# Small token tiles on TensorE: each strip of the array takes its own output columns instead of its own part of the contraction

## The chip, the cores and the metric

The kernel runs on one core of one Trainium2 chip. The metric is device time in microseconds of one execution; lower is better. Each number for a kernel is the median of several runs. Engines are named as the profile names them: PE is TensorE (PEld are its loads of the stationary operand), DVE is VectorE, ACT is ScalarE, POOL is GpSimd, SP is SyncE, which here issues most DMAs.

## What is computed

Sliding-window attention with four sink tokens, and behind it a mixture of experts with a two-level choice of one expert per token. All arrays are float32.

```python
batch, n_heads, seq, head_dim = (4, 8, 768, 64)
n_sink, window = (4, 128)
N, D, G, Eg, F = (3072, 512, 4, 4, 1024)
...
keep = is_sink | in_window
scores = np.where(keep, scores, -1000000000.0)
...
x = attn_out.transpose(0, 2, 1, 3).reshape(B * S, H * D)
...
h = np.maximum(xg[mask_e] @ w1[g, e], 0.0)
ye = h @ w2[g, e]
combined = g_w[mask_g][mask_e] * e_w[mask_e]
out[tok_idx] = combined[:, None] * ye
```

So 3072 tokens of 512 features go to 16 experts. An expert multiplies its tokens by `w1` (512 x 1024), takes the positive part, multiplies by `w2` (1024 x 512), and each row is scaled by the token's gate.

## The kernel before

The first 180 us or so hold the attention, the routing and the first expert. After that the kernel does one expert after another, in the order of the list `GROUPS`, largest first where ranks are named by size: `CAPT` gives the number of token places that the expert of each rank has (rank 3: 288, rank 8: 160, rank 14: 64, rank 15: 32). Some groups join a large and a small expert: `[3, 14]` and `[4, 15]`.

**Ordinary tiles.** Weights arrive as float32 chunks `rw` (128 x 1024, eight per expert), ACT rounds each to `whi`, and DVE subtracts to get the remainder `wlo`. Tokens, transposed by PE (`tp<-ident,xg`) and split the same way, lie in `un`. Layer 1 writes PSUM tiles `ph`, of which there are four buffers; ACT and DVE turn them into the hidden values (`hc`, `un`, `hq`). Layer 2 writes `po` (two buffers), ACT scales it by the gate into `ot`, and POOL scatters `ot` to the output rows.

**Small tiles.** Two kinds of tile hold too few tokens for that, and are multiplied in plain float32 directly from the raw chunk `rw`. One kind is the two small experts (`plain`: rank 14 with 64 tokens, rank 15 with 32), both layers. The other is the last 32 tokens of the six experts in `FEW` (ranks 3, 4, 8, 9, 10, 11), layer 2 only, from the hidden values `hq`; `rest_of` starts these, and half of the products come after the fourth hidden chunk of the tile beside them, the other half after that tile is done. With w tokens as the stationary operand a product uses w of the array's 128 columns. So `side_by_side` puts m = 128 / w products next to each other, one in each strip of w columns: strip j takes contraction chunks j, j + m, ... over all 512 output columns. Each strip ends with a partial sum of the whole output in its own partitions of PSUM, and the m partial sums have to be added: in layer 1 of a small expert ACT copies one and DVE adds the others into `hs` (lines 1018 to 1022 of the listing), in layer 2 ACT scales one into `ot` and DVE adds the others, scaled (`scalar_tensor_tensor`, lines 1072 and 1073). `hidden_t` then transposes `hs` for layer 2, in eight pieces of at most 64 rows, in two jobs.

**What sets the order.** Every instruction is kept in program order on its engine (`keep_in_program_order`, line 107). Work for the next group (transposing its tokens by `xpose`, fetching rows by `gather`, the transposes of `hidden_t`) lies in a list of jobs, `todo`. `pop_todo` counts steps of the current products and runs the next job when the count is due:

```python
        def pop_todo():
            plan["at"] += 1
            if plan["todo"] and plan["at"] >= plan["next"]:
                plan["next"] += plan["every"]
                plan["todo"].pop(0)()
```

The jobs go in pairs, and `every` is the number of counted steps `tot`, less a few, over the number of pairs. The jobs of weight splitting (`wjob`) are started by a clock that the program keeps, `spend`.

Of the kernel before, what the change touches and what calls it, by code (L numbers as in the profile page):

```python
# [10 lines left out]
F32 = mybir.dt.float32  # L11
# [4 lines left out]
AF = mybir.ActivationFunctionType  # L16
ALU = mybir.AluOpType
# [5 lines left out]
P = 128  # L23
# [4 lines left out]
DM = H * D  # L28
HP = H // 2
NDC = DM // P  # L30
G, EG, F = 4, 4, 1024
NE = G * EG
NFC = F // P
# [101 lines left out]
def moe_attention(tc, kqT, vN, vS, nsw, wgx, w1, w2, out):  # L135
    nc = Pinned(tc)
    v = nc.vector
    with ExitStack() as top, ExitStack() as att:
# [36 lines left out]
        def bank(pt):  # L175
            return pt.tile([P, 4, P], F32, name="tp")
# [11 lines left out]
        def spare():  # L188
            return tail[0].tile([P, 512], F32, name="ph")
# [48 lines left out]
        ident = const([P, P], F32, "ident")  # L238
# [231 lines left out]
        start = const([P, NE], F32, "start")  # L470
# [522 lines left out]
        def whole(*k):  # L993
            while k not in held:
                prefetch(RAW + RAWB)
                if k not in held and not wjob(True):
                    raise RuntimeError("weights out of order")
            return held[k][0]

        def side_by_side(outs, w, n, xs, ws, chunk):  # L1000
            m = P // w
            for k in range(0, n, m):
                kk = range(k, min(n, k + m))
                for u, out in enumerate(outs):
                    for j, c in enumerate(kk):
                        nc.tensor.matmul(out[j * w:(j + 1) * w], xs(c), ws(c, u), start=k == 0, stop=k + m >= n)
                for c in kk:
                    held.pop(chunk(c), None) if chunk(c) != chunk(c + 1) else None
                prefetch(RAW + RAWB)
                yield 0.46 * len(outs) * len(kk) * w / 64  # L1010

        def layer1_plain(q):
            T, r = q["T"], q["r"]
            q["hs"] = h = yp.tile([P, F], F32, name="hs", bufs=1)
            ph = [ps_h.tile([P, 512], F32, name="ph") for u in range(2)]
            yield from side_by_side(ph, T, NDC, lambda c: q["x"][:, c], lambda c, u: whole(1, r, c)[:, u * 512:(u + 1) * 512],
                                    lambda c: (1, r, c))
            for u in range(2):
                us = slice(u * 512, (u + 1) * 512)
                nc.scalar.copy(h[0:T, us], ph[u][T:2 * T])  # L1020
                for a in [a for a in range(0, P, T) if a != T]:
                    v.tensor_tensor(h[0:T, us], h[0:T, us], ph[u][a:a + T], ALU.add)

        def layer1_narrow(q):
            T, o, r = q["T"], q["o"], q["r"]
# [15 lines left out]
        def hidden_t(q, u):  # L1041
            T = q["T"]
            tx = bank(ps_t)
            for c in range(4):
                f = 4 * u + c
                nc.tensor.transpose(tx[:, c, 0:T], q["hs"][0:T, f * P:(f + 1) * P], ident[0:T, 0:T])
            if q["plain"]:
                if u == 0:
                    q["h"] = yp.tile([P, NFC, 64], F32, name="hr", bufs=1)[:, :, 0:T]
                nc.scalar.activation(q["h"][:, 4 * u:4 * u + 4], tx[:, :, 0:T], AF.Relu)  # L1050
                return
            drain(split_h(q, slice(4 * u, 4 * u + 4), tx[:, :, 0:T]))

        plan = {}
# [1 line left out]
# [5 lines that stand above are left out]
# [2 lines left out]
            yield from few_tokens(q, spare(), q["h"], q["T"], 0)  # L1063

        def few_tokens(q, po, h, T, jj):
            r = q["r"]
            yield from side_by_side([po], T, NFC, lambda f: h[:, f],
                                    lambda f, u: whole(2, r, f // 2)[:, (f % 2) * DM:(f % 2 + 1) * DM], lambda f: (2, r, f // 2))
            c = cg[r, jj]
            ot = yp.tile([P, DM], F32, name="ot", bufs=3)  # L1070
            nc.scalar.activation(ot[0:T], po[T:2 * T], AF.Copy, scale=c[0:T])
            for a in [a for a in range(0, P, T) if a != T]:
                v.scalar_tensor_tensor(ot[0:T], po[a:a + T], c[0:T], ot[0:T], ALU.mult, ALU.add)
            scatter(r, jj, T, ot)

        def scatter(r, jj, w, ot):
# [192 lines left out]
        for i, g in enumerate(PARTS):  # L1269
            nxt = PARTS[i + 1] if i + 1 < len(PARTS) else []  # L1270
            if i == 1:
                fetch(nxt)
            todo = []
            for k, q in enumerate(g):
                plan.update(todo=todo, at=0, next=2, every=2)
                if i == 0 and k == 0:
                    finish(ew)
                elif q["T"] > P:
                    finish(layer1_wide(q))
                elif q["plain"]:  # L1280
                    finish(layer1_plain(q))
                    todo = todo + [lambda q=q, u=u: hidden_t(q, u) for u in range(2)]
                else:
                    finish(layer1_narrow(q))
                    todo = todo + [lambda q=q, u=u: hidden_t(q, u) for u in range(2)]
            for f in todo if g[0]["T"] <= P else []:
                f()
                todo = []
            tot = NFC * sum((q["m"] + P - 1) // P for q in g if not q["plain"])
            if i == 0:  # L1290
                todo += [lambda: wait_for("x1"), lambda: None]
            todo += [lambda q=q, j=j: xpose(q, j) for q in nxt for j in range(q["nt"])]
            todo = [lambda fs=todo[k:k + 2]: [f() for f in fs] for k in range(0, len(todo), 2)]
            if i >= 1 and i + 2 < len(PARTS):
                todo = spread(todo, PARTS[i + 2])
            first = (4 if g[-1]["plain"] else 8) if len(g) > 1 else 2
            plan.update(todo=todo, at=0, next=first, every=(tot - first - 3) / max(1, len(todo)))
            if i == 0:
                plan.update(todo=todo[:1], next=2)
            if i + 1 == len(PARTS):  # L1300
                nc.gpsimd.drain()
                fv = nc.nc.values_load(novi[0:1, 1:2], min_val=0, max_val=MAXO)
            work = [(q, j) for q in g for j in range((q["m"] + P - 1) // P)]
            if g[-1]["plain"]:
                work.insert(1, work.pop())
            for q, j in work:
                finish(layer2_plain(q) if q["plain"] else layer2(q, j))
                if (j + 1) * P < q["m"]:
                    continue
                if i == 0 and q["r"] == 0 and not q["last"]:  # L1310
                    plan.update(todo=todo[1:], next=tot - 8, every=1.5)
            for f in plan["todo"]:
                f()
# [237 lines left out]
```

## Time and profile before

| | us |
|---|---|
| median of 3 runs | 503.58 (502.59 to 505.25) |
| the profiled execution, its own time | 505.41 |
| its span in the profile | 503.70 |
| PE busy | 483.3 |
| DVE busy | 376.9 |
| ACT busy | 328.6 |
| POOL busy | 160.8 |

A row of the profile gives engine, line, operation, output and inputs by the program's names (buffer numbers are left out), shapes as partitions x elements, and a count. Nearly all instructions have line 105, that of a helper, so tiles are told apart by name. A float32 product appears as two loads and two matmuls. Matmuls are pipelined, so the duration of one overlaps with the next; starts say how fast they go.

### The profile page before, as it was taken

The numbers are of one execution on the slowest core, as the hardware profiler recorded it, in microseconds if no ns is written. First come the engines' busy times: TensorE is split into PE (matmuls) and PEld (weight loads), VectorE is DVE, ScalarE is ACT, GpSimd is POOL, SyncE is SP. The second block draws the span as 40 slices with busy tenths as digits, with TensorE's granted clock in tenths as the row PEclk, the third lists the DMA queues.
The fourth block names the chain that finished last, engine by engine and source line by source line (L and its number), as shares of the span: only waits on it lengthen the run. The fifth ranks groups of instructions, "written<-read, shape, count | busy, mean of one in ns | idle before, by whom it ended". The sixth has DMA issues, their size and how long they took to land.

```text
span 503.7 us, 14620 instructions
## 1 busy us (share of the span) xinstructions
PE 483.3 (96%) x5399; PEld 403.1 (80%) x5399; DVE 376.9 (75%) x1175; ACT 328.6 (65%) x861; POOL 160.8 (32%) x276
## 2 busy tenths in 40 slices
PE   7998999999999999999999999899999999999994
PEld 5787888888888888989888659685768788988883
DVE  6474897899989789983174287676988888688881
ACT  4887788879895345762264276456577877677851
POOL 3564354554563012422303044120712170205021
PEclk8999999999999999999999999999999999999999
DMA  7767676877885559894123399549949996858100
GB/s 210 242 216 217 208 240 196 271 235 240 299 291 196 150 186 388 288 318 154 67 86 121 114 325 362 173 170 316 397 152 349 412 393 217 303 190 304 59 24 29
DMA packets 50000, 114.71 MB, mean 228 GB/s; under 512 B 9486, under 2 KB 9486, under 8 KB 49920
## 3 DMA queue, kind: packets, MB, share of 16 engines
q1 hardware_dynamic: 45424, 100.14, 58.3%
q0 software_dynamic: 4352, 13.26, 7.5%
q8 instruction: 44, 0.72, 0.6%
q10 hardware_dynamic: 144, 0.29, 0.3%
q14 instruction: 36, 0.29, 0.2%
HBM read 100.89 MB, written 13.24 MB: 227 GB/s over the span
## 4 chain that ended last, share of the span: by engine, by line
PE 72%; DVE 11%; issue 8%; ACT 5%; DMA 1%; POOL 1%; POOLq 0%; DVEq 0%; ACTq 0%
PE po L105 31%; PE ph L105 26%; PE ps L105 6%; PE tp L105 6%; ACT pt L105 2%; PE lg L105 2%; DVE wlo L105 2%; DVE sm L105 1%; ACT whi L105 1%; DVE ot L105 1%; DVE un L105 1%; DMA ni<-in_nsw 1%; POOL out L105 1%; DVE hs L105 1%; DVE ps L105 1%
## 5 line engine op out<-in xcount | busy, mean ns | idle before, releaser
L105 DVE TENSOR_TENSOR wlo<-rw,whi 128x1024 fp32r<-128x1024 f32 x112 | 134.5, 1223 | 25.0 <-ACT whi L105 24.4
L105 PE MATMUL ph<-un,whi 128*128 128x256 f32 (+4 forms) x576 | 132.3, 317 | 1.8 <-DVE hc L105 0.9
L105 PE MATMUL po<-whi,un 128*128 128x512 f32 (+2 forms) x384 | 127.1, 396 | 0.0
L105 ACT CAST whi<-rw 128x1024 fp32r<-128x1024 f32 (+1 forms) x116 | 115.4, 1021 | 8.0 <-PE po L105 4.7
L105 POOL DMA_INDIRECT out<-ot,sidx x33 | 43.9, 1330 | 225.4 <-ACT ot L105 156.4
L105 PE MATMUL ph<-un,wlo 128*128 128x160 f32 (+4 forms) x416 | 100.4, 266 | 0.0
L105 PEld LDWEIGHTS ph<-un,whi 128*128 128x128 f32 x576 | 94.5, 189 | 6.8 <-issue 1.7
L105 PEld LDWEIGHTS po<-whi,un 128*128 128x128 f32 (+1 forms) x384 | 70.8, 186 | 24.9 <-issue 2.5
L105 ACT ACTIVATE pt<-sm,st 128x136 f32<-128x136 f32 x192 | 76.0, 399 | 20.2 <-DVE st L105 20.1
L105 PE MATMUL po<-wlo,un 128*128 128x512 f32 (+3 forms) x200 | 78.0, 390 | 0.0
L105 PEld LDWEIGHTS ph<-un,wlo 128*128 128x128 f32 x416 | 77.1, 189 | 0.7
L105 POOL DMA_INDIRECT xg<-xd,gidx x33 | 39.0, 1183 | 35.7 <-DVE idz L105 25.2
L105 DVE CUSTOM_DVE_ANT_0 sm<-ps,msk 128x136 f32<-128x136 f32 x192 | 45.5, 295 | 3.7 <-PE ps L105 0.7
L105 PE MATMUL ps<-kb,qb 64*64 64x216 f32 (+1 forms) x768 | 41.4, 353 | 2.4 <-DMA qb<-in_kqT 2.1
L105 PEld LDWEIGHTS po<-wlo,un 128*128 128x128 f32 (+2 forms) x200 | 36.3, 182 | 7.4
L105 DVE TENSOR_TENSOR hc<-ph,hc 128x160 f32<-128x160 f32 (+2 forms) x64 | 21.9, 344 | 24.5 <-ACT hc L105 24.3
L105 ACT ACTIVATE un<-ph 128x256 fp32r<-128x256 f32 x40 | 15.4, 384 | 35.7 <-PE ph L105 35.4
L105 ACT ACTIVATION_READ_ACCUMULATOR pt<-sm,st 128x1 f32 x192 | 36.3, 189 | 0.0
L105 ACT ACTIVATE ot<-po,cg 128x512 f32<-128x512 f32 (+3 forms) x25 | 17.0, 679 | 28.0 <-PE po L105 27.9
L105 PEld LDWEIGHTS ps<-kb,qb 64*64 64x64 f32 x768 | 27.6, 139 | 9.2 <-issue 2.7
L105 ACT COPY hc<-ph 128x160 f32<-128x160 f32 (+2 forms) x64 | 19.9, 312 | 20.9 <-PE ph L105 17.5
L105 PE MATMUL po<-pa,vv 128*64 128x64 f32 x768 | 30.8, 223 | 1.6 <-issue 1.6
(199 smaller groups left out, 743.4 us busy)
## 6 DMA issues: line engine op xcount, KB each, us to landing
rw<-in_w SPq DMA_DIRECT2D x128, 512.0 KB, 5.4
vv<-in_vN SPq DMA_DIRECT2D x24, 512.0 KB, 4.5
kb<-in_kqT SPq DMA_DIRECT2D x23, 288.0 KB, 4.8
qb<-in_kqT SPq DMA_DIRECT2D x24, 256.0 KB, 4.5
xd<-xt SPq DMA_DIRECT2D x24, 256.0 KB, 2.9
svr<-in_vS SPq DMA_DIRECT2D x4, 192.0 KB, 5.3
xg<-xd,gidx POOLq DMA_INDIRECT x33, 5.2
out<-ot,sidx POOLq DMA_INDIRECT x33, 5.6
```

The lines of the kernel that those rows point to most:

```text
L105: r = f(*a, **k)
```

## The change

`side_by_side` now gives strip a of the array the output columns a·k to (a + 1)·k, with k = 512·w/128 (for layer 1, 1024·w/128), and runs it over every contraction chunk. The strips end with finished sums of different columns. A product of 32 tokens that was 512 columns wide becomes four of 128 columns, one of 64 tokens becomes two of 256 (in layer 1 of the 64-token expert the width stays 512, with both halves of the output in one PSUM tile). `layer1_plain` takes one PSUM tile instead of two and ends with one ACT copy; `hidden_t` transposes `hs` in 128-row pieces, four for 64 tokens and two for 32, and one ACT instruction puts them in place. In `few_tokens` ACT scales each strip into its columns of `ot`, and the additions on DVE are gone. Also, a half of the rest-products now counts as a step in `pop_todo`, and `tot` counts two steps for each of them.

```diff
-        def side_by_side(outs, w, n, xs, ws, chunk):
+        def side_by_side(out, w, n, k, xs, ws, chunk, plain=True):
             m = P // w
...
-                for u, out in enumerate(outs):
-                    for j, c in enumerate(kk):
-                        nc.tensor.matmul(out[j * w:(j + 1) * w], xs(c), ws(c, u), start=k == 0, stop=k + m >= n)
+                for c in kk:
+                    for a in range(m):
+                        nc.tensor.matmul(out[a * w:(a + 1) * w, 0:k], xs(c), ws(c)[:, a * k:(a + 1) * k], start=c == 0, stop=c == n - 1)
...
                 prefetch(RAW + RAWB)
-                yield 0.46 * len(outs) * len(kk) * w / 64
+                if n == NFC and not plain:
+                    pop_todo()
+                yield 0.46 * k * m / 512 * len(kk) * w / 64
...
-            for u in range(2):
-                us = slice(u * 512, (u + 1) * 512)
-                nc.scalar.copy(h[0:T, us], ph[u][T:2 * T])
-                for a in [a for a in range(0, P, T) if a != T]:
-                    v.tensor_tensor(h[0:T, us], h[0:T, us], ph[u][a:a + T], ALU.add)
+            nc.scalar.copy(h[:, 0:k], ph[:, 0:k])
...
+            if q["plain"]:
+                m = P // T
+                nb = NFC // m
+                for c in range(nb):
+                    nc.tensor.transpose(tx[:, c], q["hs"][:, c * P:(c + 1) * P], ident)
+                q["h"] = h = yp.tile([P, NFC, 64], F32, name="hr", bufs=1)[:, :, 0:T]
+                nc.scalar.activation(h.rearrange("p (a c) t -> p c a t", a=m),
+                                     tx[:, 0:nb].rearrange("p c (a t) -> p c a t", a=m), AF.Relu)
+                return
...
-            nc.scalar.activation(ot[0:T], po[T:2 * T], AF.Copy, scale=c[0:T])
-            for a in [a for a in range(0, P, T) if a != T]:
-                v.scalar_tensor_tensor(ot[0:T], po[a:a + T], c[0:T], ot[0:T], ALU.mult, ALU.add)
+            for a in range(P // T):
+                nc.scalar.activation(ot[0:T, a * k:(a + 1) * k], po[a * T:(a + 1) * T, 0:k], AF.Copy, scale=c[0:T])
...
-                    todo = todo + [lambda q=q, u=u: hidden_t(q, u) for u in range(2)]
+                    todo = todo + [lambda q=q: hidden_t(q, 0)]
...
-            tot = NFC * sum((q["m"] + P - 1) // P for q in g if not q["plain"])
+            tot = sum(NFC * ((q["m"] + P - 1) // P) + 2 * (q["m"] < q["T"]) for q in g if not q["plain"])
```

PE in layer 2 of rank 8, while the tokens of the next group `[4, 15]` are transposed (`xg` are the fetched token rows, `hq` the hidden values of the 32 rest tokens). Before:

```order
L105 MATMUL po<-whi,un 128x512
L105 MATMUL tp<-ident,xg 128x32 x8
L105 MATMUL ph<-rw,hq 32x512 x4
L105 MATMUL po<-whi,un 128x512
L105 MATMUL po<-wlo,un 128x512
```

With the change:

```order
L105 MATMUL po<-whi,un 128x512
L105 MATMUL ph<-rw,hq 32x128 x16
L105 MATMUL tp<-ident,xg 128x32 x8
L105 MATMUL po<-whi,un 128x512
L105 MATMUL po<-wlo,un 128x512
```

The first half of the rest-products, now sixteen narrow products in place of four wide ones, stands ahead of the transposes instead of behind them. The same exchange takes place in layer 2 of rank 9, with the transposes of a 128-token tile.

PE in layer 2 of `[4, 15]`, around the transposes of rank 15's hidden values `hs`. Before:

```order
L105 MATMUL po<-whi,un 128x512
L105 MATMUL tp<-ident,hs 128x32 x8
L105 MATMUL ph<-rw,hq 32x512 x4
L105 MATMUL po<-whi,un 128x512
```

With the change:

```order
L105 MATMUL po<-whi,un 128x512
L105 MATMUL tp<-ident,hs 128x128 x2
L105 MATMUL tp<-ident,xg 128x128 x4
L105 MATMUL ph<-rw,hq 32x128 x16
L105 MATMUL po<-whi,un 128x512
```

Eight transposes become two, and the transposes of the next group's 128-token tile, which stood after the products of rank 15, follow them at once.

DVE over the same stretch, from layer 1 of `[4, 15]` to layer 1 of rank 9, as the difference of the two programs:

```order
-L105 TENSOR_TENSOR hs<-hs,ph 32x512 x6
-L105 TENSOR_TENSOR wlo<-rw,whi 128x1024 x3
-L105 SCALAR_TENSOR_TENSOR ot<-ph,cg,ot 32x512 x3
-L105 TENSOR_TENSOR wlo<-rw,whi 128x1024
-L105 SCALAR_TENSOR_TENSOR ot<-ph,cg,ot 32x512 x3
-L105 TENSOR_TENSOR un<-tp,un 128x4x128
-L105 COPY cg<-xg 128x1
+L105 TENSOR_TENSOR un<-tp,un 128x4x128
+L105 COPY cg<-xg 128x1
+L105 TENSOR_TENSOR wlo<-rw,whi 128x1024 x2
 L105 TENSOR_TENSOR un<-tp,un 128x4x32
 L105 COPY cg<-xg 32x1
-L105 TENSOR_TENSOR wlo<-rw,whi 128x1024 x4
+L105 TENSOR_TENSOR wlo<-rw,whi 128x1024 x6
```

All twelve additions are gone; the eight weight splits are still there.

## Rows read from the trace of the kernel before

**Rows 1.** The page: its head, and the chain that ended last by engine.

```profile
span 503.7 us, 14620 instructions
...
PE 72%; DVE 11%; issue 8%; ACT 5%; DMA 1%; POOL 1%; POOLq 0%; DVEq 0%; ACTq 0%
```

**Rows 2.** Waits of PE, 282 to 400 us: total us, times, longest.

```profile
PE tp L105 <- DVE cg L105: 2.4, 3, 1.1
PE ph L105 <- DVE hc L105: 0.9, 2, 0.4
PE tp L105 <- DVE hs L105: 0.8, 1, 0.8
PE ph L105 <- DVE ot L105: 0.7, 1, 0.7
PE ph L105 <- DVE cg L105: 0.3, 1, 0.3
```

**Rows 3.** Busy time by stretch: PE, PEld, DVE, ACT, POOL, clock, DMA share, GB/s.

```profile
352.00:400.00 48.00, 45.15 (x259) 37.17 (x258) 42.59 (x88) 33.94 (x64) 14.51 (x10) 1.00 0.86 323
400.00:488.00 88.00, 88.00 (x506) 74.19 (x505) 74.06 (x145) 66.49 (x122) 23.66 (x16) 1.00 0.64 227
```

**Rows 4.** Timeline of layer 2 of `[4, 15]`: start, us, engine, instruction [idle before].

```profile
340.73 2.12 DVE L105 TENSOR_TENSOR hs<-hs,ph 32x512 f32<-32x512 f32 x3
...
342.90 0.43 PE L105 MATMUL tp<-ident,hs 32*128 32x32 f32 x4 [0.85 <-DVE hs L105]
...
343.26 1.07 PE L105 MATMUL ph<-rw,hq 128*32 128x512 f32 x8
```

**Rows 5.** Timeline of layer 2 of rank 8.

```profile
317.68 0.43 PE L105 MATMUL tp<-ident,xg 32*128 32x32 f32 x4 [1.13 <-DVE cg L105]
...
318.34 0.43 PE L105 MATMUL tp<-ident,xg 32*128 32x32 f32 x4 [0.23 <-DVE cg L105]
...
318.70 1.07 PE L105 MATMUL ph<-rw,hq 128*32 128x512 f32 x8
...
319.70 0.50 PE L105 MATMUL po<-whi,un 128*128 128x512 f32 x1
```

**Rows 6.** Timeline of rank 9 and of layer 1 of rank 6.

```profile
357.01 4.61 DVE L105 TENSOR_TENSOR wlo<-rw,whi 128x1024 fp32r<-128x1024 f32 x4
...
361.90 0.41 PE L105 MATMUL ph<-un,whi 128*128 128x320 f32 x1 [0.45 <-DVE hc L105]
...
371.82 0.65 PE L105 MATMUL tp<-ident,xg 128*128 128x128 f32 x4 [1.04 <-DVE cg L105]
...
381.75 0.41 PE L105 MATMUL ph<-un,whi 128*128 128x384 f32 x1 [0.65 <-DVE ot L105]
```

**Rows 7.** Instructions that write `ot`: duration ns min/median/max, first and last start, forms.

```profile
L105 DVE SCALAR_TENSOR_TENSOR ot<-ph,cg,ot x22: 732/745/754, 295.1 to 496.4; 32x512 f32<-32x512 f32 x21, 64x512 f32<-64x512 f32 x1
L105 ACT ACTIVATE ot<-ph,cg x9: 473/681/686, 294.4 to 494.9; 32x512 f32<-32x512 f32 x7, 64x512 f32<-64x512 f32 x1, 128x256 f32<-128x256 f32 x1
```

**Rows 8.** Timeline of the last rest-products (rank 11).

```profile
492.62 0.13 PEld L105 LDWEIGHTS ph<-rw,hq 128*32 128x32 f32 x4 [0.30 <-issue]
493.05 0.13 PEld L105 LDWEIGHTS ph<-rw,hq 128*32 128x32 f32 x4 [0.30 <-issue]
```

**Rows 9.** Loads of those products: duration ns min/median/max.

```profile
L105 PEld LDWEIGHTS ph<-rw,hq x96: 106/109/111, 289.2 to 493.1; 128*32 128x32 f32 x96
```

**Rows 10.** Timeline of the attention's 64-column products, two strips side by side.

```profile
100.89 0.64 PE L105 MATMUL po<-pa,vv 128*64 128x64 f32 x16
101.36 0.64 PE L105 MATMUL po<-pu,vv 128*64 128x64 f32 x16
```

**Rows 11.** Timeline of the end.

```profile
494.87 2.31 DVE L105 SCALAR_TENSOR_TENSOR ot<-ph,cg,ot 32x512 f32<-32x512 f32 x3 [4.12 <-ACT ot L105]
...
497.15 0.47 ACT L105 ACTIVATE ot<-po,cg 128x256 f32<-128x256 f32 x1 [1.81 <-PE po L105]
497.46 0.87 POOL L105 DMA_INDIRECT out<-ot,sidx  x1 [12.42 <-DVE ot L105]
498.63 0.99 POOL L105 DMA_INDIRECT out<-ot,sidx  x1 [0.30 <-issue]
```

More of the change, by code (lines that the diff above doesn't have):

```diff
@@ L998, in whole @@
             return held[k][0]
-        def side_by_side(outs, w, n, xs, ws, chunk):
+        def side_by_side(out, w, n, k, xs, ws, chunk, plain=True):
             m = P // w
-            for k in range(0, n, m):
-                kk = range(k, min(n, k + m))
-                for u, out in enumerate(outs):
-                    for j, c in enumerate(kk):
-                        nc.tensor.matmul(out[j * w:(j + 1) * w], xs(c), ws(c, u), start=k == 0, stop=k + m >= n)
+            for k0 in range(0, n, m):
+                kk = range(k0, min(n, k0 + m))
+                for c in kk:
+                    for a in range(m):
+                        nc.tensor.matmul(out[a * w:(a + 1) * w, 0:k], xs(c), ws(c)[:, a * k:(a + 1) * k], start=c == 0, stop=c == n - 1)
                 for c in kk:
@@ L1009, in side_by_side @@
                 prefetch(RAW + RAWB)
-                yield 0.46 * len(outs) * len(kk) * w / 64
+                if n == NFC and not plain:
+                    pop_todo()
+                yield 0.46 * k * m / 512 * len(kk) * w / 64
         def layer1_plain(q):
             T, r = q["T"], q["r"]
+            k = F * T // P
             q["hs"] = h = yp.tile([P, F], F32, name="hs", bufs=1)
-            ph = [ps_h.tile([P, 512], F32, name="ph") for u in range(2)]
-            yield from side_by_side(ph, T, NDC, lambda c: q["x"][:, c], lambda c, u: whole(1, r, c)[:, u * 512:(u + 1) * 512],
-                                    lambda c: (1, r, c))
-            for u in range(2):
-                us = slice(u * 512, (u + 1) * 512)
-                nc.scalar.copy(h[0:T, us], ph[u][T:2 * T])
-                for a in [a for a in range(0, P, T) if a != T]:
-                    v.tensor_tensor(h[0:T, us], h[0:T, us], ph[u][a:a + T], ALU.add)
+            ph = spare()
+            yield from side_by_side(ph, T, NDC, k, lambda c: q["x"][:, c], lambda c: whole(1, r, c), lambda c: (1, r, c))
+            nc.scalar.copy(h[:, 0:k], ph[:, 0:k])
         def layer1_narrow(q):
@@ L1046, in hidden_t @@
                 nc.tensor.transpose(tx[:, c, 0:T], q["hs"][0:T, f * P:(f + 1) * P], ident[0:T, 0:T])
[L1047 to L1051, printed above, removed]
             drain(split_h(q, slice(4 * u, 4 * u + 4), tx[:, :, 0:T]))
@@ L1065, in few_tokens @@
         def few_tokens(q, po, h, T, jj):
-            r = q["r"]
-            yield from side_by_side([po], T, NFC, lambda f: h[:, f],
-                                    lambda f, u: whole(2, r, f // 2)[:, (f % 2) * DM:(f % 2 + 1) * DM], lambda f: (2, r, f // 2))
+            r, k = q["r"], DM * T // P
+            yield from side_by_side(po, T, NFC, k, lambda f: h[:, f],
+                                    lambda f: whole(2, r, f // 2)[:, (f % 2) * DM:(f % 2 + 1) * DM], lambda f: (2, r, f // 2), q["plain"])
             c = cg[r, jj]
             ot = yp.tile([P, DM], F32, name="ot", bufs=3)
-            nc.scalar.activation(ot[0:T], po[T:2 * T], AF.Copy, scale=c[0:T])
-            for a in [a for a in range(0, P, T) if a != T]:
-                v.scalar_tensor_tensor(ot[0:T], po[a:a + T], c[0:T], ot[0:T], ALU.mult, ALU.add)
+            for a in range(P // T):
+                nc.scalar.activation(ot[0:T, a * k:(a + 1) * k], po[a * T:(a + 1) * T, 0:k], AF.Copy, scale=c[0:T])
             scatter(r, jj, T, ot)
```

## The prediction

> **What bounds the kernel now.** The page comes first: of the chain that ended last PE holds 72% and DVE 11% [rows 1]. So an operation taken off DVE is worth something only where PE, or the last output, waits for DVE. The second view is the list of PE's waits in the stretch in which small tiles are computed. It is short, and every entry names DVE: 2.4 + 0.9 + 0.8 + 0.7 + 0.3 = 5.1 us, five groups, eight waits [rows 2]. The third is busy time by stretch. From 352 to 400 us DVE works 42.59 of 48 us, from 400 to 488 PE is busy all of 88.00 us [rows 3]; what DVE saves in the later stretch shortens nothing there. The timelines then show what stands in each wait, and the end of the kernel has a queue of its own on POOL.
>
> **What the change does to the products.** It leaves the multiplications and the columns streamed through each strip as they were, and makes more and narrower instructions of them. Half of a 32-token contraction (call it a block: four chunks, four strips) was two passes of 512 columns in each strip and becomes eight of 128. There are 14 such blocks: two for each of the six rest tiles, two for layer 2 of rank 15. One pass of 512 columns takes 493.05 - 492.62 = 0.43 us [rows 8]. No row has 128 columns, so I bound it. From above: the attention's 64-column products, two strips at a time, start 16 in 101.36 - 100.89 = 0.47 us, 0.029 us each [rows 10]; if instructions can't be fed faster than that, the 32 of a block take 0.94 us against 2 x 0.43 = 0.86, 0.08 more. From below: strictly by columns, nothing more. Between: a straight line through 64 columns (0.47/8 = 0.059 in one strip) and 512 (0.43) gives 0.059 + 64 x 0.00083 = 0.112 for 128, 0.90 for a block, 0.04 more. I take the line, as both its ends are measured with strips running together: 14 x 0.04 = 0.5, and 0.1 for the 256-column products of the two small experts. **Cost 0.6 us, between 0 and 1.2.** [...]
>
> **What it takes off, place by place.**
>
> *Hidden values of rank 15.* DVE adds six partial sums; three take 2.12 us [rows 4]. PE stands 0.85 us before the second four of eight transposes, and that second four last until 343.26, another 0.36 us [rows 4]. Afterwards one ACT copy feeds two transposes; it starts when layer 1 ends, with four counted steps of layer 2 between, so it is not late. Gain 0.85 + 0.36 = **1.2 us** (0.85 to 1.3). For rank 14 the profile names no such wait: 0. The next tile's transposes move up in both groups; between nothing and 0.3 us for one interruption of layer 2 less, I take nothing.
>
> *Rank 8.* The transposes of the last small tiles wait 1.13 and 0.23 us for DVE to empty a PSUM tile [rows 5]. Only then does the first rest block run, from 318.70 to 319.70, 1.00 us. The change counts steps differently, and the block now stands ahead of these transposes: it runs in the wait. The transposes can start no earlier than now, but the ordinary products follow them at once. Gain **1.0 us** (0 if the DVE work moves along, 1.0 at most).
>
> *Rank 9.* The same exchange at a wait of 1.04 us [rows 6]. Gain **1.0 us** (same bounds). The transposed tile comes no earlier, while layer 1 after it does; a later wait there is part of the first rival.
>
> *Layer 1 of rank 6.* PE waits 0.65 us because the three additions of a rest tile stand ahead of `hc` on DVE [rows 6], 0.745 us each [rows 7]. They go. In their place ACT does four strips of 128 columns instead of one of 512. From 0.681 for 512 and 0.473 for 256 [rows 7] a line gives 0.37 for 128, so 4 x 0.37 - 0.68 = 0.8 us more on ACT, per rest tile. Queued behind it are ACT's own `hc` copy and weight casts. With four `ph` buffers PE can run ahead of that. Gain **0.6 us** (between 0.65 and a loss of 0.15, the 0.8 exposed).
>
> *Layer 1 of rank 9.* Two waits of 0.45 us for `hc` (one in [rows 6], the sum in [rows 2]) and one of 0.3 for `cg`. DVE is late there: four splits run back to back for 4.61 us [rows 6] after 6 x 0.71 + 6 x 0.745 = 8.7 us of additions in the group before [rows 4, 7], all of which go. But the splits also need weights that have landed, and DMA engines are at 0.86 [rows 3]. Of 1.2 us I take half, **0.6 us** (0 to 1.2).
>
> *The end.* POOL's second-last scatter starts at 497.46, 0.28 after DVE's last addition (494.87 + 2.31 = 497.18), and ends at 498.33. The last starts 0.30 later, though its data are ready at 497.15 + 0.47 = 497.62 [rows 11]. Without additions, ACT begins the rest tile about 0.68 ahead of DVE's first addition, at 494.2, ends four strips at 495.7 and so lets POOL run from 496.0 to 496.9. The last scatter then waits only for its data: 497.62 + 0.28 = 497.9 instead of 498.63. Gain **0.7 us** (0 to 0.7).
>
> Other removed additions lie where PE waits for nothing: 0, with PE's own products as cover. **Sum:** 1.2 + 1.0 + 1.0 + 0.6 + 0.6 + 0.7 - 0.6 = 4.5 us. The profiled execution took 505.41 us with a span of 503.70; less 4.5 that makes 500.9. It was 1.8 us slower than the median of the runs, 503.58, from which the same sum gives **499.1 us**, 0.9% less. A difference of 0.5%, 2.5 us, is about what a measurement can tell from none. With every upper bound the gain is 1.3 + 1.0 + 1.0 + 0.65 + 1.2 + 0.7 + 0.6, with no cost for narrow products, 6.4 us: 497.2.
>
> **Rivals.** *The waits move on.* PE gets ahead of DVE by the exchange alone, not by faster evictions, and may meet weights or ACT at the next place. For it: DVE at 42.59 and ACT at 33.94 of 48 us, DMA at 0.86 [rows 3], and 0.8 us more ACT work for each rest tile. Against it: no wait in [rows 2] names ACT or a DMA. Then the four gains at ranks 8, 9 and 6 (3.2 us) are given back, and 503.58 - (1.2 + 0.7 - 0.6) = 502.3 remains, between 501 and 503.
>
> *Loads become visible; the other sign.* Each strip now gets a new stationary tile for every 128 columns instead of 512: eight loads per block and strip, where there were two. If a strip's load waits for its own product, 0.109 us [rows 9] is exposed in each of 14 x 8 passes: 12.2 us, so 499.1 + 12.2 = 511.3. The 4.5 us are used up once 0.040 us of each load shows, and it is slower by over 0.5% from 0.063. [...]
>
> *Feeding binds.* [...] By the slowest feeding that rows show it costs 14 x 0.08 = 1.1 us, which is in my range; to be slower overall it would need 0.038 us per instruction instead of 0.029 [rows 10]. [...]
>
> *It does not do what it says.* The additions go, but the waits belong to something that the profile names wrongly, such as a transfer behind DVE's wait. Then gains and cost cancel: 503.6. Against it: at the places above DVE is seen working up to the end of PE's wait.
>
> **Chances.** Forecast 0.66, of which all is faster by over 0.5%; waits move on 0.20, of which 0.05 still faster and 0.15 the same; not what it says 0.06, the same; loads visible 0.06 and feeding 0.02, slower. So faster 0.71, same 0.21, slower 0.08. The range goes from 497.0, just below all upper bounds, to 502.8, which takes in most of the first rival; 0.08 + 0.06 and a little of the rival, some 0.17, lie outside. The forecast alone would reach from 497.0 to 501.0.
>
> **What would show it.** Right: `hq` blocks of about 0.9 us with 128-column matmuls some 0.11 apart in a strip; the transposes of rank 8 and 9 behind a block, with a wait under 0.4 us; two `hs` transposes without wait; no `ot` addition on DVE before `hc`; the last scatter starting within 0.3 us of its data. Wrong: blocks of 1.2 us or more, waits of PE for `whi`, `wlo` or ACT between 340 and 400 us, or a stretch from 400 to 488 us that has grown.

## The result and the profile after

The changed kernel takes **496.94 us** (median of four runs, 495.42 to 498.27) against 504.41 of the kernel before in the same comparison: ratio 0.9854, 95% interval 0.981 to 0.9898, so 7.5 us less. Forecast were 499.1 us, 4.5 less. The sign is as forecast; the size is not, and 496.94 lies 0.06 under the low end of the range. A later comparison found a smaller gain, 4.7 us; it comes under "Before, order and change once more".

The profiled execution took 497.12 us. Its page, to be held against [rows 1]:

```profile
span 495.4 us, 15313 instructions
...
PE 479.5 (97%) x5757; PEld 412.5 (83%) x5757; DVE 354.9 (72%) x1145; ACT 331.8 (67%) x879; POOL 154.9 (31%) x276
...
PE 76%; issue 7%; DVE 6%; ACT 5%; DMA 3%; POOL 1%; POOLq 0%; ACTq 0%; DVEq 0%
```

DVE's share of the chain has fallen from 11% to 6%. The waits of PE from 282 to 400 us, before five groups with 5.1 us [rows 2]:

```profile
PE ph L105 <- DVE hc L105: 0.4, 1, 0.4
PE tp L105 <- DVE cg L105: 0.2, 1, 0.2
```

Busy time by stretch, with the columns of [rows 3]. No wait went into the later stretch. From 352 to 400 us ACT works 39.09 us where it had 33.94, but these microseconds hold other work now that the kernel is ahead; over the whole kernel ACT has 331.8 us instead of 328.6:

```profile
352.00:400.00 48.00, 47.59 (x326) 40.97 (x325) 41.53 (x86) 39.09 (x73) 11.48 (x10) 1.00 0.92 351
400.00:488.00 88.00, 88.00 (x632) 77.09 (x631) 66.15 (x140) 62.65 (x125) 20.04 (x14) 1.00 0.54 193
```

Timeline of layer 2 of rank 8, which answers to [rows 5]. The 32 narrow products run where PE stood for 1.13 us, and the first four transposes follow them without a listed wait; by the starts 0.2 us of it is left (1.20 us from the block to the transposes, where a block takes 1.01). The wait of 0.23 us ahead of the second four is the one that stayed:

```profile
313.76 1.08 PE L105 MATMUL ph<-rw,hq 128*32 128x128 f32 x32
...
314.96 0.43 PE L105 MATMUL tp<-ident,xg 32*128 32x32 f32 x4
...
315.62 0.43 PE L105 MATMUL tp<-ident,xg 32*128 32x32 f32 x4 [0.23 <-DVE cg L105]
...
315.98 0.50 PE L105 MATMUL po<-whi,un 128*128 128x512 f32 x1
```

Timeline of PE in layer 2 of `[4, 15]`, which answers to [rows 4]: two `hs` transposes with no wait, and the next tile's transposes and the rest-products in one piece behind them.

```profile
337.58 0.39 PE L105 MATMUL po<-whi,un 128*128 128x512 f32 x1
337.81 0.38 PE L105 MATMUL tp<-ident,hs 128*128 128x128 f32 x2
338.03 0.60 PE L105 MATMUL tp<-ident,xg 128*128 128x128 f32 x4
338.56 1.08 PE L105 MATMUL ph<-rw,hq 128*32 128x128 f32 x32
339.57 0.50 PE L105 MATMUL po<-whi,un 128*128 128x512 f32 x1
```

From 338.56 to 339.57 are 1.01 us for a block (products are counted as the rows count them, two for one in float32); from 318.70 to 319.70 it was 1.00 with wide products [rows 5]. The end, which answers to [rows 11]:

```profile
485.51 1.98 ACT L105 ACTIVATE ot<-ph,cg 32x128 f32<-32x128 f32 x5 [3.76 <-PE ph L105]
...
487.27 0.88 POOL L105 DMA_INDIRECT out<-ot,sidx  x1 [12.10 <-ACT ot L105]
...
488.51 0.47 ACT L105 ACTIVATE ot<-po,cg 128x256 f32<-128x256 f32 x1 [1.02 <-PE po L105]
489.26 1.00 POOL L105 DMA_INDIRECT out<-ot,sidx  x1 [1.11 <-ACT ot L105]
```

The last scatter starts 489.26 - 488.98 = 0.28 us after its data, where it was 1.01 [rows 11].

**Place by place.** The table below is read from the starts of PE's products: the time from one stage's first product to the next stage's, in microseconds. The last column, called the measure in the expectations, runs from the first layer-2 product of `[3, 14]` to the first product behind the last rest tile. It leaves out the start and the end of the kernel, whose durations vary between executions. The rows for the experiments are used below; a repeat stands as "again".

| kernel | [3,14] L2 | 8 L2 | [4,15] L2 | 9 L1 | 9 L2 | 6 L1 | measure |
|---|---|---|---|---|---|---|---|
| before | 18.89 | 10.98 | 18.46 | 9.76 | 10.55 | 15.70 | 208.4 |
| after | 18.54 | 10.00 | 16.62 | 8.88 | 9.37 | 14.78 | 202.2 |
| order alone | 18.85 | 9.99 | 18.12 | 10.59 | 9.37 | 15.70 | 206.7 |
| products alone | 18.75 | 12.55 | 16.67 | 8.25 | 10.58 | 14.77 | 205.5 |
| layer 2 and order | 18.92 | 10.00 | 18.19 | 9.90 | 9.37 | 14.78 | 205.1 |
| layer 1 and order | 18.49 | 9.99 | 16.53 | 10.63 | 9.35 | 15.70 | 204.8 |
| 64-column products | 18.58 | 10.02 | 16.66 | 8.98 | 9.38 | 14.77 | 202.4 |
| one block | 18.41 | 9.91 | 16.46 | 8.23 | 9.48 | 14.66 | 200.7 |
| before, again | 18.89 | 12.53 | 18.46 | 9.77 | 10.55 | 15.70 | 210.0 |
| products alone, again | 18.75 | 12.58 | 16.67 | 8.23 | 10.58 | 14.77 | 205.5 |
| before, third | 18.89 | 12.55 | 18.46 | 9.77 | 11.27 | 15.71 | 210.7 |
| order alone, again | 18.85 | 9.99 | 18.12 | 10.61 | 9.35 | 15.71 | 206.7 |
| after, again | 18.54 | 10.00 | 20.13 | 8.24 | 9.37 | 14.77 | 205.0 |
| after, third | 18.54 | 10.00 | 20.10 | 8.23 | 9.37 | 14.77 | 205.0 |

Between the first two profiles 6.3 us of the measure go. The two executions differ by 505.41 - 497.12 = 8.3 us: 6.3 there, 2.4 already ahead of rank 14's first product, where both kernels run the same work, and 0.4 given back at the end. The 2.4 belong to the executions and not to the change: in its second profile the kernel before was only 0.3 us behind at that point (279.92 us against 279.63), and order alone came there at 281.72 and 283.07. In the first profile of the kernel before the granted clock of PE was at 0.50 for some 3.4 us near 48 us, but that doesn't explain them: in the second profile of order alone the clock of the whole span is 0.998 on the mean, against 0.992 there, and it is the latest of all.

### The profile page after: what moved, and what is told of

Its sections match the earlier page's. It is cut to its first block, busy times and chain, and to the rows that moved or that the text cites. A ratio compares the mean times of both kernels' runs of the same rounds, so it can differ in the third digit from the quotient of the medians.

```text
span 495.4 us, 15313 instructions
## 1 busy us (share of the span) xinstructions
PE 479.5 (97%) x5757; PEld 412.5 (83%) x5757; DVE 354.9 (72%) x1145; ACT 331.8 (67%) x879; POOL 154.9 (31%) x276
## 4 chain that ended last, share of the span: by engine, by line
PE 76%; issue 7%; DVE 6%; ACT 5%; DMA 3%; POOL 1%; POOLq 0%; ACTq 0%; DVEq 0%
PE po L105 33%; PE ph L105 28%; PE tp L105 7%; PE ps L105 6%; PE lg L105 3%; ACT pt L105 3%; DMA rw<-in_w 2%; DVE sm L105 1%; ACT whi L105 1%; DMA ni<-in_nsw 1%; DVE wlo L105 1%; POOL out L105 1%; DMA xg<-xd,gidx 1%; DVE un L105 1%; DVE ps L105 1%
## 5 line engine op out<-in xcount | busy, mean ns | idle before, releaser
L105 POOL DMA_INDIRECT out<-ot,sidx x33 | 41.4, 1254 | 224.4 <-ACT ot L105 136.5
L105 POOL DMA_INDIRECT xg<-xd,gidx x33 | 35.6, 1079 | 35.4 <-DVE idz L105 24.9
L105 PE MATMUL ps<-kb,qb 64*64 64x216 f32 (+1 forms) x768 | 40.1, 345 | 2.3 <-DMA qb<-in_kqT 2.0
L105 POOL TENSOR_SCALAR_AFFINE_SELECT pu<-pa 64x512 f32<-64x512 f32 x40 | 27.8, 695 | 14.2 <-ACT pa L105 14.0
```

What stands on the lines that cost most here:

```text
L105: r = f(*a, **k)
```

## The experiments

Theory: PE's waits for DVE were the price, some paid back by the additions' going (products), some by the exchange at ranks 8 and 9 (order). Rivals: the waits move on; narrow products cost loads or feeding time.

### Order alone, products alone

Order alone is the kernel before with two edits (and the argument `plain` handed through):

```diff
                 prefetch(RAW + RAWB)
+                if n == NFC and not plain:
+                    pop_todo()
...
-            tot = NFC * sum((q["m"] + P - 1) // P for q in g if not q["plain"])
+            tot = sum(NFC * ((q["m"] + P - 1) // P) + 2 * (q["m"] < q["T"]) for q in g if not q["plain"])
```

> The kernel before, with only the counting of steps changed (a half of a rest tile's products counts as a step, two more steps in tot). Measure: from the first layer-2 product of the group [3, 14] to the first product behind the last rest tile, 208.42 us before and 202.16 with the change. Theory (the exchange of order alone lets a rest block run in DVE's wait at ranks 8 and 9): 1.0 us less at each, 206.4. Rival (the waits move on while DVE still has its additions): the two waits shrink but come back before layer 1 of rank 4 or 6, 207.5 to 208.4.

Measured: 502.01 us against 504.85, ratio 0.9938 (0.9914 to 0.9963), measure 206.7, near the theory's 206.4. Ranks 8 and 9 give their 0.99 and 1.18 us and layer 2 of `[4, 15]` another 0.34, but layer 1 of rank 9 gets 0.83 us longer. The waits of PE, 282 to 405 us, and the timeline of the longest:

```profile
PE ph L105 <- DVE hc L105: 1.8, 2, 1.4
PE tp L105 <- DVE hs L105: 0.8, 1, 0.8
PE ph L105 <- DVE ot L105: 0.6, 1, 0.6
PE tp L105 <- DVE cg L105: 0.2, 1, 0.2
```

```profile
359.37 0.34 PE L105 MATMUL ph<-un,whi 128*128 128x320 f32 x1
361.09 0.41 PE L105 MATMUL ph<-un,whi 128*128 128x320 f32 x1 [1.37 <-DVE hc L105]
```

For the order by itself the first rival is therefore right in part: PE gets ahead and meets DVE one layer later, where the waits for `hc` grow from 0.9 to 1.8 us, and a third of the gain goes back.

Products alone is the changed kernel with those two edits taken back.

> The change without the counting of steps: the order of transposes and rest blocks at ranks 8 and 9 is the old one, the quarter products and the missing additions stay. Same measure. Theory (the exchange of order holds 2.0 of the 6.3 us): 204.2. Rival (the additions taken off DVE shorten these waits by themselves, the order adds nothing): 202.2 to 202.7, with waits under 0.3 us at the transposes of ranks 8 and 9.

Measured: 499.89 us, ratio 0.9896 (0.9864 to 0.9928). One group of waits is left, and not one of its three has become shorter:

```profile
PE tp L105 <- DVE cg L105: 2.4, 3, 1.1
```

So the additions' going doesn't help the transposes of ranks 8 and 9, and the exchange doesn't help `hs`, `hc` and `ot`. Only the short wait for `cg` ahead of rank 9's layer 1, 0.3 us in [rows 2], goes with either. Both parts of the theory stand. But the measure was to be 204.2 and is 205.5, and the whole excess lies in layer 2 of rank 8. Busy time by stretch there (the granted clock is the third number from the right):

```profile
316.00:320.00 4.00, 4.00 (x42) 3.09 (x43) 1.62 (x4) 1.21 (x2) 0.00 (x0) 0.60 0.47 148
```

PE's timeline of the same place:

```profile
315.26 0.43 PE L105 MATMUL tp<-ident,xg 32*128 32x32 f32 x4 [1.13 <-DVE cg L105]
315.92 0.43 PE L105 MATMUL tp<-ident,xg 32*128 32x32 f32 x4 [0.23 <-DVE cg L105]
316.28 1.47 PE L105 MATMUL ph<-rw,hq 128*32 128x128 f32 x32
317.68 0.80 PE L105 MATMUL po<-whi,un 128*128 128x512 f32 x1
```

Behind the two waits with thin transposes between them the granted clock is 0.60 on the mean from 316 to 320 us, and 0.97 in the next four. At the 0.50 of the kernel before near 48 us these two means make some 3.4 us, an estimate. The block takes 1.40 us instead of 1.01, and the stage 12.55 instead of 10.98. The kernel before has the same waits and had kept its clock in its first profile, 1.00 from 310 to 326 us. Two repeats followed.

> The kernel before, unchanged, profiled once more: how much of the 2.38 us by which the changed kernel was ahead before its first small product repeats. Theory (nothing that the change touches runs there; the profile of before had the clock at half for 3.41 us at 48 us, which fell elsewhere in the changed one): the first product of rank 14 starts anywhere from 279.6 to 282.1 us, and earlier than 281 where no such stretch is seen after 11 us. Rival (the changed program is faster there): 281.7 to 282.1 again, whatever the clock does. The measured span stays 208.4.

Measured: 505.34 us in one run. Layer 2 of rank 8 takes 12.53 us, and the measure is 210.0, 1.6 above what was expected.

> The change without the counting of steps, profiled once more. In its first profile the clock was at half for 3.41 us right behind the wait at rank 8, and layer 2 of rank 8 took 12.55 us instead of 10.98 before with the same wait. Theory (whether the clock falls there differs between executions; the wait alone costs what it did): 10.9 to 11.0 us if the clock stays up, about 12.5 if it falls; measured span then 204.0 or 205.5. Rival (narrow products behind the wait are slow there by themselves): 12.5 with the clock up.

Measured: 500.78 us in one run, and 12.58 us at rank 8.

### Before, order and change once more

> The kernel before, unchanged, profiled a third time, for the clock at rank 8. With the old order the clock fell to half right behind the wait at rank 8 in three of four profiles, with the new order in none of six. Theory (PE's wait of 1.13 us there, with only thin transposes around it, is what lets the clock fall, in most executions): layer 2 of rank 8 takes about 12.5 us with the clock at half for a stretch at 316 to 318 us, three times in four; else 10.98. Rival (chance): no preference between the orders, so about three in ten.

> The kernel before with only the counting of steps changed, profiled again, for the clock at rank 8. Theory (the rest block fills the wait): no fall of the clock between 290 and 400 us, layer 2 of rank 8 takes 10.0 us. Rival (chance): a fall there about three times in ten, and then 11.5.

> The changed kernel, unchanged, profiled again, for the clock at rank 8 and for the end. Theory: no fall of the clock between 290 and 400 us, measured span 202.2 us as in the first profile; the last scatter starts 0.27 us after its data are ready, and is done later after that than in the profiles with the old layer 2. Rival (chance): a fall there about three times in ten, and the end as short as with the old layer 2.

Measured, one run each on one chip: 506.59, 504.83 and 501.35 us, with a kernel before that took 507.89 there. The third profile of the kernel before shows the fall again:

```profile
316.00:320.00 4.00, 3.77 (x19) 1.90 (x20) 2.28 (x6) 1.48 (x3) 0.00 (x0) 0.66 0.34 90
```

With the transposes ahead of the block the clock fell in four of five profiles (before 2 of 3, products alone 2 of 2: means of 0.60 and 0.66 over four microseconds in two of them, a stage of 12.53 and 12.58 us in the two others); with the block ahead of them in none of nine (a stage of 9.91 to 10.02 us). It costs 12.55 - 10.98 = 1.57 us each time. So the order is worth 0.98 us at rank 8 by its wait, and 1.57 more where the clock falls. That this is the cause rests on these counts and on the place. The third profile of the kernel before has a column of its own kind too, 11.27 us at rank 9, where the wait for `cg` ahead of the transposes is 1.8 us instead of 1.0; why is not shown. Order alone repeats its first profile to 0.02 us in every column. The changed kernel doesn't: layer 2 of `[4, 15]` takes 20.13 us instead of 16.62.

> The changed kernel once more, timed against the kernel before in five rounds and with a third profile of it. Measure: from the first layer-2 product of [3, 14] to the first product behind the last rest tile; 202.16 us in its first profile, 204.99 in its second, of which 2.83 us were gaps of PE without a releaser (issue, up to 0.5 us each) among the narrow products of rank 15. Theory: the gaps belong to that chip and call, where the kernel before and the order alone had gaps of 0.4 and 0.8 us too; on another chip the measure is 202 to 202.6, PE has no gap put down to issue between 280 and 400 us, and the time is 0.982 to 0.988 of the kernel before. Rival: narrow products meet such gaps in most executions; then they come again, the measure is 204 to 206, and the ratio lies above 0.988. The clock at rank 8 is full in both. The single block of rest-products (0.9821, 495.26 us) is better than the changed kernel if the ratio here is above 0.984.

Measured on the fourth chip of the experiments: 501.53 us (500.31 to 503.84, six runs) against 506.26, ratio **0.9917** (0.9885 to 0.9949). The theory that such gaps belong to one chip has fallen: they are there again, at the same instructions. PE's timeline of rank 15's layer 2, first in this run and then in the first profile of the same kernel:

```profile
344.59 1.08 PE L105 MATMUL ph<-rw,hq 128*32 128x128 f32 x32
345.60 0.43 PE L105 MATMUL tp<-ident,xg 32*128 32x32 f32 x4
345.96 1.33 PE L105 MATMUL ph<-rw,hr 128*32 128x128 f32 x35
347.74 0.41 PE L105 MATMUL ph<-rw,hr 128*32 128x128 f32 x3 [0.45 <-issue]
348.49 0.43 PE L105 MATMUL ph<-rw,hr 128*32 128x128 f32 x5 [0.34 <-issue]
349.25 0.41 PE L105 MATMUL ph<-rw,hr 128*32 128x128 f32 x3 [0.33 <-issue]
349.98 0.47 PE L105 MATMUL ph<-rw,hr 128*32 128x128 f32 x5 [0.32 <-issue]
350.75 0.66 PE L105 MATMUL ph<-rw,hr 128*32 128x128 f32 x13 [0.29 <-issue]
351.34 0.50 PE L105 MATMUL po<-whi,un 128*128 128x512 f32 x1
```

```profile
342.57 1.08 PE L105 MATMUL ph<-rw,hq 128*32 128x128 f32 x32
343.58 0.43 PE L105 MATMUL tp<-ident,xg 32*128 32x32 f32 x4
343.94 1.96 PE L105 MATMUL ph<-rw,hr 128*32 128x128 f32 x64
345.83 0.50 PE L105 MATMUL po<-whi,un 128*128 128x512 f32 x1
```

The 64 products take 345.83 - 343.94 = 1.89 us in one and 5.38 in the other. After 32 + 4 + 35 narrow products and transposes at full rate PE waits for nothing that the profile names, gets a few, and waits again, five times, some 0.75 us from one start to the next. The second profile breaks off after the same 35. The 3.5 us bring back 0.65 in layer 1 of rank 9, where DVE has caught up (8.88 to 8.23); 2.8 us net remain, about the difference between the gains of 7.5 and 4.7 us. The other twelve blocks, and rank 14's 256-column products, run without gaps. The gaps stand in two profiles of two chips. Six have the same 64 products without gaps, in 1.9 us: five experiments on two other chips, and the first profile of the changed kernel, whose chip is not known. What differs is not shown. Over the eight microseconds with the gaps the clock is full (1.00), and the DMA share is 0.79 and 1.01, against 0.74 and 1.01 over the eight from the same block on in the first profile. That instructions come late from memory would be a guess, and the trace doesn't support it: the packets of the instruction queue nearest to the gaps of this run stand between 342 and 343 us and between 352 and 353, none between those. What the engine holds in the meantime is not recorded.

### Layer 2 alone, layer 1 alone, each with the order

Layer 2 alone is the changed kernel with layer 1 of the small experts, and `hidden_t`, as before:

```diff
-            ph = spare()
-            yield from side_by_side(ph, T, NDC, k, lambda c: q["x"][:, c], lambda c: whole(1, r, c), lambda c: (1, r, c))
-            nc.scalar.copy(h[:, 0:k], ph[:, 0:k])
+            ph = [ps_h.tile([P, 512], F32, name="ph") for u in range(2)]
...
+                for a in [a for a in range(0, P, T) if a != T]:
+                    v.tensor_tensor(h[0:T, us], h[0:T, us], ph[u][a:a + T], ALU.add)
```

> The change in layer 2 alone: layer 1 of the two small experts as before, with partial sums added on DVE and eight small transposes. Same measure. Theory: the wait for hs in [4, 15] comes back, 0.85 us, and four transposes more, 0.36, so 1.2 us and up to 0.7 for DVE's later splits at rank 9: 203.4 to 204.1. Rival (what counted at [4, 15] is the later additions, not those of layer 1): under 0.5 us, 202.6.

Measured: 499.32 us, ratio 0.9885 (0.9823 to 0.9947), measure 205.1, above what the theory allowed. The `hs` wait of 0.8 us stands again, and layer 2 of `[4, 15]` takes 18.19 - 16.62 = 1.57 us more than in the changed kernel. Layer 1 of rank 9 takes 9.90 - 8.88 = 1.02 us more, where 0.7 was the most expected, and layer 2 of `[3, 14]` 0.38 more.

Layer 1 alone has `few_tokens` as before:

```diff
-            for a in range(P // T):
-                nc.scalar.activation(ot[0:T, a * k:(a + 1) * k], po[a * T:(a + 1) * T, 0:k], AF.Copy, scale=c[0:T])
+            nc.scalar.activation(ot[0:T], po[T:2 * T], AF.Copy, scale=c[0:T])
+            for a in [a for a in range(0, P, T) if a != T]:
+                v.scalar_tensor_tensor(ot[0:T], po[a:a + T], c[0:T], ot[0:T], ALU.mult, ALU.add)
```

> The change in layer 1 alone: layer 2 of the small tiles as before (partial sums over parts of the contraction, DVE adds them), the new counting of steps kept. Same measure. Theory: the wait of 0.65 us for hc in layer 1 of rank 6 comes back, and part of the 0.9 us at layer 1 of rank 9; wide products are 0.02 us per block cheaper: 203.0 to 203.6. The last scatter starts 0.7 us later after the last product than with the change. Rival (only layer 1's additions mattered): 202.2 or less.

Measured: 500.34 us, ratio 0.99 (0.9846 to 0.9954), measure 204.8, above the theory's 203.0 to 203.6. The waits of PE:

```profile
PE ph L105 <- DVE hc L105: 1.8, 2, 1.4
PE ph L105 <- DVE ot L105: 0.7, 1, 0.7
PE tp L105 <- DVE cg L105: 0.2, 1, 0.2
```

With layer 2's additions back, 10.63 us at layer 1 of rank 9 (8.88 in the changed kernel) and 15.70 at rank 6 (14.78) are back too. At rank 6 the price was layer 2's additions alone: with layer 1's back it stays at 14.78. At rank 9 it was both: 10.63 with layer 2's additions back, 9.90 with layer 1's. The theory had only a part of 0.9 us there, and 1.75 came.

### Narrower still

```diff
+                z = 64 if n == NFC and not plain else k
                 for c in kk:
-                    for a in range(m):
-                        nc.tensor.matmul(out[a * w:(a + 1) * w, 0:k], xs(c), ws(c)[:, a * k:(a + 1) * k], start=c == 0, stop=c == n - 1)
+                    for z0 in range(0, k, z):
...
```

> The change with each 128-column product of the rest tiles cut into two of 64 columns, so 64 products in a block instead of 32. Measure: from the first product of such a block to the first instruction of another kind behind it (1.01 us with the change at layer 2 of [4, 15], 0.99 before). Theory (products run at the speed of their columns plus a few ns each): 16 passes of 0.059 in a strip, 0.94 instead of 0.87, so about 1.08 us. Rival (loads are hidden only just, or feeding binds near 0.027 us per instruction): 64 x 0.027 is 1.7 us or, with loads of 0.109 showing, over 2 us.

Measured: 496.62 us in one run, measure 202.4. PE's timeline of the same place as above:

```profile
338.51 1.10 PE L105 MATMUL ph<-rw,hq 128*32 128x64 f32 x64
339.54 0.50 PE L105 MATMUL po<-whi,un 128*128 128x512 f32 x1
```

Twice the products and twice the loads take 1.03 us where 32 took 1.01. Loads thus stay hidden, one every 0.016 us, though each lasts some 0.109 [rows 9]; the second rival has fallen. These strips share all rows, and twice the loads cost 0.02 us.

### One block of rest-products

```diff
                 if rest and f == 3:
-                    yield next(rest)
+                    yield from rest
```

> The change with both halves of a rest tile's products run in one block after the fourth hidden chunk, for all rest tiles but the last (which has that already). Same measure of the span from the first layer-2 product of [3, 14] to the first product behind the last rest tile, 202.16 us with the change. Theory: going into and out of a block costs about 0.4 us (0.33 instead of 0.23 ahead of it, 0.31 instead of 0.11 behind it, 0.34 instead of 0.23 for the next product), saved five times: 200.2. Rival (the chunks of the second half are then needed 2.8 us earlier and PE waits for them): 202 or more, with waits for weights or DMA.

Measured: **495.26 us** (494.8 to 496.4, six runs) against 504.46, ratio 0.9821 (0.9793 to 0.985), measure 200.7. All rest-products of a tile follow one another, and one interruption of layer 2 goes:

```profile
337.82 1.95 PE L105 MATMUL ph<-rw,hq 128*32 128x128 f32 x64
339.71 0.50 PE L105 MATMUL po<-whi,un 128*128 128x512 f32 x1
```

64 products take 1.89 us, 0.13 less than two blocks of 1.01. Layer 1 of rank 9 takes 8.23 us instead of 8.88, as its last wait is gone. This version beats the kernel before, and its median is 1.7 us below the first one of the changed kernel; the intervals of the two ratios overlap. It was not run on a chip on which the changed kernel had its gaps, so whether it keeps its lead there is open. In it 64 narrow products at most follow one another, with up to six transposes ahead of them, while the gaps began after 71 products and transposes; whether that avoids them is not shown.

## Why the prediction was right, and where it was not

**Direction and mechanism: right.** PE's waits for DVE held the time, and the additions and the order each removed those that the prediction gave them: `hs`, `hc` and `ot` the first, `cg` at the transposes the second. The short wait for `cg` ahead of rank 9's layer 1 goes with either. Most gains were put too low.

**The waits are worth more than the list says.** The profile counts a wait from the modelled end of the product before, but pipelined products start well ahead of that end. In order alone the starts around the wait of 1.37 us are 1.72 apart (359.37 and 361.09), where such a pair usually follows within 0.19: 1.53 were lost. The same can be read in the kernel before. These are the starts ahead of its waits; the starts behind `hs`, `hc` and `ot` stand in [rows 4] and [rows 6]:

```profile
341.62 0.43 PE L105 MATMUL tp<-ident,hs 32*128 32x32 f32 x4
...
356.42 0.40 PE L105 MATMUL po<-whi,un 128*128 128x512 f32 x1
357.08 0.42 PE L105 MATMUL ph<-un,whi 128*128 128x320 f32 x1 [0.26 <-DVE cg L105]
...
361.11 0.34 PE L105 MATMUL ph<-un,whi 128*128 128x320 f32 x1
...
380.74 0.36 PE L105 MATMUL ph<-un,whi 128*128 128x384 f32 x1
```

| wait | listed | lost by the starts |
|---|---|---|
| `hs`, rank 15 | 0.85 | 342.90 - 341.62, less 0.36 for four transposes: 0.92 |
| `cg`, ahead of rank 9 | 0.26 | 357.08 - 356.42, less 0.24 as in the changed kernel: 0.42 |
| `hc`, rank 9, twice | 0.45 | 361.90 - 361.11, less the usual 0.19: 0.60 each |
| `ot`, rank 6 | 0.65 | 381.75 - 380.74, less the usual 0.20: 0.81 |

So the step of the sum that took listed idle time for the time lost was 0.07 to 0.16 us short at each wait. Layer 1 of rank 6 was put at 0.6 and gave 0.92. Rank 9's two waits for `hc`, 0.9 in the list, are worth 1.51 in products alone. Part of what the starts leave open lies right behind the waits, where products also start further apart (361.90 to 362.16, where 0.18 is usual).

**Rank 15's hidden values: 1.2 forecast, 1.5 came; what lies above it is mostly the transposes.** The wait gives 0.92. Of the eight transposes the forecast counted four as spared, 0.36 us; but eight took 0.72 without the wait, and two take 0.22 (337.81 to 338.03). The step into them is 0.10 shorter too (0.23 instead of 0.33 us). That makes 1.52; layer 2 alone is 1.57 slower than the changed kernel in this column. For rank 14, where there is no wait, the shorter transposes were put at nothing, and 0.35 came in its column: they take 0.43 us instead of 0.64, and the step into them is 0.10 shorter again. It goes with layer 1's part of the change (18.49 in layer 1 and order, 18.92 in layer 2 and order).

**The transposes that move up were put at nothing, but end a wait.** In order alone they give 0.34 in layer 2 of `[4, 15]`: rank 9's tokens are ready earlier, and its first product no longer waits for `cg`. The forecast had this wait in its list for layer 1 of rank 9. In the table it falls into the column before, since it stands ahead of the first product.

**Rank 9's exchange: 1.0 forecast as the most possible, 1.18 came.** The bound was the time of the block itself. What it left out is the step behind the transposes: 372.41 - 371.82 = 0.59 us when a block follows them, as before, and 0.41 when an ordinary product does, as with the change:

```profile
365.40 0.66 PE L105 MATMUL tp<-ident,xg 128*128 128x128 f32 x4
365.81 0.48 PE L105 MATMUL po<-whi,un 128*128 128x512 f32 x1
```

**Layer 1 of rank 9: 0.6 forecast, twice that came.** Its column gives 0.88, and the wait for `cg` another 0.42 in the column before: 1.3, above the upper bound of 1.2. Half was taken because the splits also need weights that have landed. That held nothing up: in products alone PE has no wait left in this layer. What took a part back was the order, 0.83 against 1.51. So the first rival is real at this one place, and is outweighed.

**The range: an upper bound with a slip.** 1.3 + 1.0 + 1.0 + 0.65 + 1.2 + 0.7 is 5.85 us with no cost for narrow products; the 0.6 us of that cost was added on top, which gave 6.4. The bounds as stated lead to 497.7, not 497.2. That 496.94 lies so near the low end of 497.0 is in part owed to this slip.

**Rank 8: 1.0 forecast, 0.98 read, and a term that was missing.** The clock that fell behind these waits in four of five profiles cost 1.57 us more. The one profile ahead of the prediction did not show it. By these counts it is about 1.2 us on average, and the largest single reason why the medians differ by 7.5 us and not by some 6.

**Narrow products: 0.6 forecast, about 0.2 or about 3.** Where they run freely a block is 0.015 us longer (14 of them: 0.2), less than the line through two widths gave. In two profiles, however, one stretch has gaps, 2.8 us net, above the upper bound of 1.2. If what is missing there is instructions, which is not shown, the third rival, that feeding binds, is partly true, though not as it was put: no fixed time per instruction, as 64-column products at twice the number show, but gaps of 0.3 to 0.5 us after 71 narrow products and transposes.

**The end: 0.7 forecast, the start right, the landing not.** In all eight profiles with the new layer 2 the last scatter starts 0.27 to 0.28 us after its data, in all six with the old one 1.01. But from the data to the end of the span pass 5.2 to 6.5 us (mean 5.94) with the new and 6.1 to 6.6 (mean 6.33) with the old. So about 0.4 of 0.73 are kept on average, and none in the first profile. Why a scatter that starts earlier lands so unevenly stays open.

**ACT: right.** The strips of 32 x 128 take 0.36 us where 0.37 was expected, and ACT is named in no wait of PE from 282 to 400 us.

Sum of the first profile, by the table: 0.98 + 1.84 + 0.88 + 1.18 + 0.92 + 0.35 for `[3, 14]` + 0.1 elsewhere = 6.3 us, then about 1.2 for the clock (1.57 in four of five) and some 0.4 for the end, 7.9; measured were 7.5.

## What to carry to other kernels

Give the strips of the array output columns rather than parts of the contraction: on TensorE that cost 0.015 us for a block of 32 where they ran freely, and the engine that added the partial sums is freed where TensorE waits for it. Price a wait by the starts around it, not by the idle time that is listed, and put independent products into it: that fills the wait and may keep the clock up, as it did in nine of nine profiles here (layer 2 of rank 8 in 9.91 to 10.02 us, not 12.53 to 12.58). Before relying on many narrow products in a row, profile them on more than one chip, and look for gaps that no engine ends.

## What was not expected of the hardware

- Behind waits of 1.13 and 0.23 us with thin transposes between them the granted clock fell in four of five profiles (0.60 and 0.66 on the mean of four microseconds in two, a stage of 12.53 and 12.58 us in the others), and in none of nine where a block of rest-products filled the first wait.
- The same 64 narrow products at one place took 1.9 us in six profiles and 5.4 us in two, of two chips, with the first gap at the same product.
- A stationary tile every 0.016 us, in strips that share all rows, cost 0.02 us in a block of 1.03 us.
